# A fused cross-attention and maxout kernel: seven output pieces at the end, states-stationary scores, DMA-turned states and a new order

## Chip, cores and metric

The kernel runs on one core of one Trainium2 chip. The metric is the device time of one execution in microseconds (us). The engines are called as the profile calls them: PE (TensorE, matmuls; PEld its weight loads), DVE (VectorE), ACT (ScalarE), POOL (GpSimd) and SP (SyncE, which here only issues DMAs). Each engine works through its own queue of instructions in the order in which the program lists them, and waits on semaphores for what others produce.

## The reference

Two blocks run after each other. The first is a cross attention between tokens and a few states, with one softmax in each direction, and the second is a maxout feed-forward layer over the result.

```
B, H, S, Ns, D = 8, 8, 512, 32, 64
scores  = (x @ state^T) / sqrt(D);  a  = softmax(scores);   xread = a  @ state      # [B,H,512,64]
scores2 = (state @ x^T) / sqrt(D);  a2 = softmax(scores2);  sread = a2 @ x          # [B,H, 32,64]
y = concat([xread, sread], axis=2) -> rows of 8*64 = 512 features                   # 4352 rows
h = max(y @ w1, y @ w2, y @ w3)                                                     # 768 features
out = h @ w_out                                                                     # float32, 4352 x 512
```

Inputs and output are float32; the kernel computes in bf16 with float32 sums.

## The kernel before

**The work.** Eight batches of 512 token rows are computed one after the other, with the work of neighbouring batches interleaved, and at the end the 256 state rows of all batches together. The product of the attention with the states is folded into the weights: instead of `(a @ state) @ w` the kernel computes `G = state @ w` for each batch (three matrices of 768 columns for each of two halves of the heads, 4608 columns in all) and then `a @ G`. So each batch has these steps, and each step has a short name in the order table:

- `lx`, `lxg`, `lxu`: load x, all heads, half of them, or half without a cast; `lst`: load two batches' states; `lw`, `lwo`: load weights.
- `xt`/`xtc` or `xtd`: turn (transpose) x on PE with a copy out, or by DMA from SP. `stc`, `stt`, `stp`: cast two batches' states, turn them on PE, place the turned states into the block-diagonal tile `bd`. `std` is a DMA in place of `stt`, there in the code before but not in the order.
- `sc`, `ex`: the scores of tokens against states, 16 matmuls with x as the standing weights, and the exponential on ACT. `sq`, `eq`, `etd`: the same scores with the states as the standing weights (the result lies turned), their exponential, and a DMA that turns the exponentials into the layout of `e`. These three are also there in the code before but not in the order.
- `sum`, `wt`: row sums and reciprocal on DVE; the weights `a`, mostly on POOL. `at`/`atc` or `atd`: turn `a` on PE or by DMA.
- `pad`, `sr`, `srs`, `srt`, `ap`: the other softmax direction, that is a padded copy of x on POOL, 32 small matmuls, a scaling on DVE, a DMA turn from SP, and a placement into the tile that holds all batches' state rows.
- `g`/`gc`, `gr`/`gq`/`grc`: a slice or a run of columns of `G` on PE in 64x32 array tiles, and the copy out of PSUM. Letters at the end of a step name the engine or engines (`A` ACT, `D` DVE, `P` POOL, `S` SP).
- `l1`, `m0`, `ma`, `mb`: layer one, six matmuls into three PSUM banks for 128 of the 768 features; then a copy of the first bank on ACT and two maxima on DVE. `l1s` is the same for the state rows.
- `l2`, `l2c`, `so`: layer two, six matmuls into one bank for 128 rows, the copy out, the store. `l2p`, `l2pc`, `sop` do the same for a range of the 512 output columns; they are used at the end of the program.
- `busy`: one matmul on zeros, to keep PE running at the start. `look` and `flag`: at the end the kernel checks that all softmax sums were in range. `look` works on DVE; `flag` is a small matmul (L575), a reduction (L577) and a comparison (L578) on DVE. `vl` (L583) then loads the flag into a register of each engine, and a branch (L674) skips a slow repeat of everything. `hold` is one more matmul on zeros and a copy (L591, L593).

**What sets the order.** Nothing is scheduled by rules: the string `PLAN` lists all steps in one order, and each engine's queue is that order cut down to its own instructions. `BANKS` and `PAIRS` say which PSUM bank each request gets, and `PLACES` which of the two to four SBUF buffers a tile gets. A step waits for the last reader of its bank or buffer.

**PSUM.** Before, four banks are given out singly and four in two pairs; a pair takes the scores of a batch or two runs of `G`, and then one instruction copies 1024 columns out of it.

**DMA queues.** POOL issues the loads of x and of the weights and most stores; SP issues the turns and a few stores; ACT loads the states and issues a few late stores. A DMA is issued only when the engine's queue reaches it and what it waits for is there.

**The end.** The last batch's output is computed in 12 pieces of 128 or 256 columns and the first half of the state rows' output in two.

Of the kernel before, what the change touches and what calls it, by code (L numbers as in the profile page):

```python
# [9 lines left out]
F32 = mybir.dt.float32  # L10
# [8 lines left out]
    lst 0 A; lxu 0 0 S; zero; clr 0; clr 1; clr 2; clr 3; warm; lxg 0 1; busy 1; xones 1; ident; busy 1;  # L19
    lxg 1 0; busy 1; busy 1; stc 0 D; busy 1; busy 1; busy 1; busy 1; busy 1; lxg 1 1; stt 0; busy 1; busy 1;  # L20
    cxu 0 0 D; xt 0 0; stp 0 A; busy 1; xt 0 1; lw 0 2 1; lw 0 1 0; xtc 0 0 D; sc 0 0; xones 0; lw 0 2 2;
    xtc 0 1 D; busy 1; busy 1; sc 0 1; xt 1 0; ex 0 0; ex 0 1; lw 1 3 0; sum 0 0; sum 0 1; xtc 1 0 A; busy 1;
    busy 1; xt 1 1; sc 1 0; xtc 1 1 D; ex 1 0; busy 1; busy 1; sc 1 1; lw 2 3 2; wt 0 1 D; lw 2 3 1; lw 3 4 0;
    wt 0 0 P; lw 3 6 2; at 0 0; sr 0; ex 1 1; sr 1; g 0 0; sum 1 0; wt 1 0 P; g 1 0; atc 0 0 A; at 0 1; at 1 0;
    gc 0 0 A; atc 0 1 A; g 1 1; sum 1 1; gc 1 0 D; atc 1 0 A; srs 0; srs 1; g 0 1; wt 1 1 P; at 1 1; gc 0 1 A;
    l1 0 0; atc 1 1 D; lst 1 A; m0 0 0; lst 3 A; gc 1 1 A; ma 0 0; lw 3 6 1; lw 4 6 0; lxg 2 1; lxg 2 0; l1 0 1;
    m0 0 1; lwo; mb 0 0; g 0 2; g 1 2; ma 0 1; l1 1 0; lst 2 A; gc 0 2 A; mb 0 1; m0 1 0; ma 1 0; l1 0 2;
    mb 1 0; gc 1 2 A; m0 0 2; ma 0 2; l1 1 1; m0 1 1; g 1 3; stc 1 P; mb 0 2; ma 1 1; g 0 3; mb 1 1; stt 1;
    gc 1 3 A; l1 1 2; gc 0 3 A; m0 1 2; stp 1 DA; ma 1 2; g 0 4; g 0 5; l1 0 3; gc 0 5 D; g 1 4; mb 1 2;
    gc 0 4 A; m0 0 3; gc 1 4 A; ma 0 3; gr 2 1792 2304; mb 0 3; l1 1 3; m0 1 3; grc 2 1792 2304 A; xtd 2;  # L30
    ma 1 3; l1 0 5; stc 2 P; g 1 5; gr 2 0 512; mb 1 3; m0 0 5; ma 0 5; l1 1 4; gc 1 5 A; gr 2 1280 1792;
    m0 1 4; grc 2 0 512 D; mb 0 5; gr 2 512 1024; ma 1 4; grc 2 1280 1792 AD; l1 0 4; m0 0 4; ma 0 4; stt 2;
    mb 0 4; sc 2 -; ex 2 -; grc 2 512 1024 D; stp 2 AD; stc 3 D; mb 1 4; l2 0 3; l2 0 0; l2c 0 3 A; l2c 0 0 A;
    sum 2 -; l2 0 1; ones; pad 2; lxg 3 0; lxg 3 1; wt 2 - P; stt 3; xtd 3; l2c 0 1 A; l1 1 5; pad 3;
    so 0 0 2 P; lx 4; m0 1 5; l2 0 2; ma 1 5; mb 1 5; stp 3 A; l2c 0 2 A; l2 1 0; gq 2 1024 1280; gr 3 0 512;
    gr 3 1792 2304; l2c 1 0 D; grc 3 1792 2304 D; gqc 2 1024 1280 A; grc 3 0 512 A; atd 2; sr 2; l2 1 1; srs 2;
    sc 3 -; l1 2 0; m0 2 0; ex 3 -; l2c 1 1 D; l2 1 3; ma 2 0; gq 3 1024 1280; so 0 2 4 P; gqc 3 1024 1280 A;
    l2c 1 3 A; gr 3 512 1024; gr 3 1280 1792; mb 2 0; sum 3 -; wt 3 - P; atd 3; xtd 4; srt 0; sr 3; srs 3;
    l1 2 1; m0 2 1; ma 2 1; l1 2 2; m0 2 2; mb 2 1; ma 2 2; l1 2 3; m0 2 3; mb 2 2; ma 2 3; l1 2 5; m0 2 5;
    mb 2 3; l2 1 2; grc 3 1280 1792 A; grc 3 512 1024 A; ma 2 5; mb 2 5; l2c 1 2 D; l1 2 4; so 1 2 4 P; m0 2 4;  # L40
    ma 2 4; lx 5; mb 2 4; so 1 0 2 P; pad 4; gr 4 1792 2304; gr 4 0 512; grc 4 1792 2304 AD; l2 2 0; l2 2 1;
# [38 lines left out]
    1032103210 3213201321 0312013201 3201320120 3120132103 1203120312 0310321031 2013210321 0321032132 0132103120  # L80
    1320132103 2103120120 1201320123 0123120123 0213012013 0130123102 2
"""
PAIRS = """
    0101010101 1001010010 0110101010 1010101010 10
"""
PLACES = """
# [657 lines left out]
```

## Time and profile before

| what | before |
|---|---|
| time, median of 3 executions | 152.52 us (152.26 to 152.56) |
| profiled execution, from the first to the last instruction | 150.5 us |
| time of the runs beyond that span | 2.0 us |
| PE busy | 145.1 us (96%) |
| DVE busy | 118.0 us (78%) |
| ACT busy | 83.2 us (55%) |
| POOL busy | 56.1 us (37%) |
| granted TensorE clock | 1.000 |
| moved by DMA | 22.29 MB, mean 148 GB/s |

The span does not hold what lies around the program on the chip, so a time is read as span plus 2.0 us. "Busy" leaves out register, branch and semaphore instructions; these are seen only when a line of the program is asked for by itself. In rows of groups, the two numbers behind `|` are the busy time in us and the mean duration of one instruction in ns. In the chain of waits each row gives the start, the length and the work that the end of the program had to wait for, in us.

### The profile page before, as it was taken

Reading aid. Unit: us, or ns where it says so; the run is one execution under the profiler, and the core shown is the slowest. Engines: PE = TensorE matmul, PEld = TensorE weight load, DVE = VectorE, ACT = ScalarE, POOL = GpSimd, SP = SyncE. Lnnn points to the kernel's source line nnn. Section 1 sums busy time; section 2 is a strip of 40 time slices with the busy share of each in tenths; the row PEclk is TensorE's granted clock in tenths of the full one; section 3 lists DMA queues with packets and bytes.
Section 4 is the critical chain, followed back from the end, with each engine's and each line's share of the span. In section 5 each row is a group of like instructions: output and inputs, shape, how many; then the busy total and the mean of one; then the engine's idle time right before and its main releaser. Section 6 shows DMA issues by size and latency. Waiting matters only on the chain.

```text
span 150.5 us, 3618 instructions
## 1 busy us (share of the span) xinstructions
PE 145.1 (96%) x1422; PEld 72.8 (48%) x1422; DVE 118.0 (78%) x202; ACT 83.2 (55%) x144; POOL 56.1 (37%) x78
## 2 busy tenths in 40 slices
PE   6998999999999999999999999999999999999991
PEld 2556443335444443444344434443444446689770
DVE  6488788999967899789978997899789888674443
ACT  3366888965654574457546764676466653332220
POOL 6996911090392507350735064506250200001500
PEclk9999999999999999999999999999999999999999
DMA  4999999949647996998399839983303340300555
GB/s 121 195 188 189 206 230 198 196 97 139 124 97 171 235 182 189 108 209 178 145 102 216 183 139 90 231 183 131 157 4 78 121 175 7 139 0 17 190 199 167
DMA packets 39108, 22.29 MB, mean 148 GB/s; under 512 B 23072, under 2 KB 36896, under 8 KB 39088
## 3 DMA queue, kind: packets, MB, share of 16 engines
q0 software_dynamic: 15872, 13.96, 49.3%
q1 hardware_dynamic: 21632, 6.69, 22.8%
q10 hardware_dynamic: 1584, 1.38, 3.2%
q8 instruction: 12, 0.20, 0.6%
q14 instruction: 8, 0.07, 0.2%
HBM read 15.20 MB, written 8.91 MB: 160 GB/s over the span
## 4 chain that ended last, share of the span: by engine, by line
PE 88%; DMA 5%; POOL 3%; issue 1%; DVE 1%; ACT 1%; POOLq 0%
PE pw L477 47%; PE po L514 25%; PE pg L427 6%; DMA w<-in_moe_w_dram 5%; PE po L532 4%; PE ps L305 2%; PE psr L391 2%; POOL w L217 1%; POOL x L206 1%; PE pgh L427 1%; ACT G L444 1%; PE pt L261 1%; DVE held L593 0%; PE idle L591 0%; PE pat L358 0%
## 5 line engine op out<-in xcount | busy, mean ns | idle before, releaser
L477 PE MATMUL pw<-aT,G 128*128 128x512 bf16 x288 | 66.7, 379 | 0.0
L492 ACT CAST t<-pw 128x512 bf16<-128x512 f32 (+1 forms) x54 | 30.5, 564 | 27.3 <-PE pw L477 26.4
L497 DVE TENSOR_TENSOR t<-t,pw 128x512 bf16<-128x512 bf16 (+1 forms) x54 | 35.3, 654 | 11.1 <-ACT t L492 8.9
L477 PEld LDWEIGHTS <-G 128*128 128x128 bf16 x288 | 27.1, 98 | 32.8 <-issue 2.1
L514 PE MATMUL po<-wout,ht 128*128 128x512 bf16 x168 | 39.7, 379 | 0.0
L505 DVE TENSOR_TENSOR ht<-t,pw 128x512 bf16<-128x512 bf16 x48 | 32.9, 686 | 4.5
L349 POOL TENSOR_TENSOR a<-e,rden 128x1024 bf16<-128x1024 bf16 (+1 forms) x9 | 14.6, 1622 | 27.2 <-ACT osb L526 11.1
L514 PEld LDWEIGHTS <-ht 128*128 128x128 bf16 x168 | 15.4, 98 | 19.0 <-issue 1.7
L548 POOL DMA_DIRECT2D out_dram<-osb x13 | 7.4, 571 | 27.5 <-ACT t L492 27.5
L466 ACT CAST G<-pg 128x1024 bf16<-128x1024 f32 (+1 forms) x17 | 14.7, 895 | 2.1 <-PE pg L427 2.1
L526 ACT COPY osb<-po 128x512 f32<-128x512 f32 x15 | 8.9, 592 | 9.1 <-PE po L514 9.1
L526 DVE COPY osb<-po 128x512 f32<-128x512 f32 x14 | 9.6, 688 | 3.9 <-PE po L514 3.8
L375 POOL COPY xp<-x 128x1024 bf16<-128x1024 bf16 x12 | 12.3, 1059 | 0.0
L313 ACT ACTIVATE e<-ps 128x1024 bf16<-128x1024 f32 (+1 forms) x10 | 8.5, 854 | 6.7 <-PE ps L305 6.7
L466 DVE CAST G<-pg 128x1024 bf16<-128x1024 f32 (+1 forms) x12 | 11.6, 995 | 0.0
L342 DVE TENSOR_REDUCE seen<-e 128x32 f32<-128x1024 bf16 (+1 forms) x10 | 10.0, 997 | 1.7 <-ACT e L313 1.7
L427 PE MATMUL pg<-w,bd 64*32 64x512 bf16 (+1 forms) x288 | 10.7, 362 | 0.4 <-DMA w<-in_moe_w_dram 0.2
L444 ACT CAST G<-pg 128x768 bf16<-128x768 f32 x10 | 8.0, 810 | 2.7 <-PE pg L427 2.5
L543 POOL DMA_DIRECT2D out_dram<-osb x4 | 2.2, 544 | 19.4 <-ACT osb L537 19.4
L249 PE MATMUL idle<-zero 128*128 128x512 bf16 x18 | 7.4, 506 | 1.8 <-DVE zero L225 1.3
L477 PE MATMUL pw<-atp,w 128*128 128x256 bf16 x72 | 8.7, 272 | 0.0
L217 POOL DMA_DIRECT2D w<-in_moe_w_dram x10 | 7.7, 782 | 0.0
(70 smaller groups left out, 112.1 us busy)
## 6 DMA issues: line engine op xcount, KB each, us to landing
out_dram<-osb POOLq DMA_DIRECT2D x12, 512.0 KB, 3.7
x<-in_x_dram POOLq DMA_DIRECT2D x4, 512.0 KB, 7.2
x<-in_x_dram POOLq DMA_DIRECT2D x7, 256.0 KB, 5.8
w<-in_moe_w_dram POOLq DMA_DIRECT2D x4, 256.0 KB, 7.5
w<-in_moe_w_dram POOLq DMA_DIRECT2D x2, 384.0 KB, 7.5
wout<-in_moe_w_out_dram POOLq DMA_DIRECT2D x1, 768.0 KB, 12.0
out_dram<-osb SPq DMA_DIRECT2D x3, 256.0 KB, 2.4
stf<-in_state_dram ACTq DMA_DIRECT2D x4, 128.0 KB, 5.3
```

The lines of the kernel that those rows point to most:

```text
L342: nc.vector.reduce_sum(out=den, in_=parity(e[b], g), axis=AX.X)
L349: times[c](out=parity(a[b], g).rearrange("p j g s n -> p j (g s) n"), in0=parity(e[b], g).rearrange("p j g s n -> p j (g s) n"), in1=rdens ...
L375: nc.gpsimd.tensor_copy(out=xp[b][:, :, :, g * (D + 1):g * (D + 1) + D], in_=v[:, g])
L427: nc.tensor.matmul(p(s, g), bd(b, 2 * s + g)[64 * g:64 * g + 64, g, :], f(w_sb[64 * g:64 * g + 64, s]), start=True, stop=True, tile_positi ...
L444: copier[c[g]](out=G[b][:, g:h, :, m * 128:m * 128 + 128], in_=p[:, g:h, 0:384].rearrange("p g (i f) -> p g i f", i=3))
L466: copier[c[g]](out=v[:, g:h], in_=p[:, g:h, 0:c1 - c0])
L477: nc.tensor.matmul(pw[i][:, 0:n], lhs(i, k), rhs(k), start=(k == 0), stop=(k == nk - 1))
L492: nc.scalar.copy(out=t0s[b, m][:, 0:n], in_=open_ps["l", b, m][0][:, 0:n])
L497: nc.vector.tensor_max(t1s[b, m][:, 0:n], t0s.pop((b, m))[:, 0:n], open_ps["l", b, m][1][:, 0:n])
L505: nc.vector.tensor_max(ht[b][:, m, :], t1s.pop((b, m))[:, 0:n], open_ps.pop(("l", b, m))[2][:, 0:n])
L514: nc.tensor.matmul(p, ht[b][:, m, tokens(b, j)], wout_sb[:, m, :], start=(m == 0), stop=(m == NM - 1))
L526: copier[c[i]](out=o[:, j, i * w:i * w + w], in_=p[:, i * w:i * w + w])
```

## The change

Six things are changed at once:

1. **The end.** Batch 7's output is computed in 7 pieces of 128 to 512 columns, the first half of the state rows' output in one.
2. **Scores of batches 4 to 7** use `sq`, `eq`, `etd` in place of `sc`, `ex`.
3. **States 4 to 7** (the pairs 2 and 3) are turned by `std`, a DMA from SP, in place of `stt` on PE.
4. **PSUM**: all eight banks are given out singly. The scores and each pair of runs of `G` take two banks, and two instructions copy them out. `gq` is gone, since all `gr` now work like it.
5. **The padded copy of x** has its two halves 66 columns apart instead of 65, and its column of ones is two columns wide.
6. **All orders are new**: `PLAN`, `BANKS` and `PLACES`. Among other things there are 25 `busy` instead of 18, 14 of them ahead of the first turn of states instead of 9; `flag` is the fourth step from the end instead of the 44th; and the stores of whole rows are spread over POOL, SP and ACT, so that POOL issues 30 DMAs instead of 39.

```diff
 PLAN = """
-    lst 0 A; lxu 0 0 S; zero; clr 0; clr 1; clr 2; clr 3; warm; lxg 0 1; busy 1; xones 1; ident; busy 1;
+    zero; lxu 0 0 S; xones 1; busy 1; busy 1; lxg 0 1; busy 1; lst 0 A; busy 1; busy 1; ident; xones 0; busy 1;
...
-    sop 7 0 256 384 S; hold; vl;
+    flag; sop 7 1 0 384 S; hold; vl;
 """
...
-    homes = {n: iter("".join(t.split())) for n, t in (("b", BANKS), ("w", PAIRS))}
+    homes = [iter("".join(BANKS.split()))]
...
     def scores(b, g=None):
+        if g is None:
+            ps = [bank([128, 2, 2, HS, Ns], F32, "ps") for _ in range(2)]
...
     def exps(b, g=None):
...
+        if g is None:
+            for i in range(2):
+                nc.scalar.activation(
+                    out=out[:, i], in_=ps[i].rearrange("p c g s n -> p c (g s n)"), func=AF.Exp, scale=scale)
...
     def scores_turned(b):
-        p = open_ps["sq", b] = two_banks([128, 2, 2, 2, 128], F32, "pst")
+        ps = open_ps["sq", b] = [bank([128, 2, 2, 128], F32, "pst") for _ in range(2)]
...
     def exps_turned(b):
         new(eT, b, [128, 2 * J * 128], "eT")
-        nc.scalar.activation(
-            out=eT[b], in_=open_ps.pop(("sq", b)).rearrange("q c i g t -> q (c i g t)"), func=AF.Exp, scale=scale)
+        for c, p in enumerate(open_ps.pop(("sq", b))):
+            nc.scalar.activation(
+                out=eT[b][:, c * 512:c * 512 + 512], in_=p.rearrange("q i g t -> q (i g t)"), func=AF.Exp, scale=scale)
...
-    def g_run(b, c0, c1, apart=False):
...
+    def g_run(b, c0, c1):
+        ps = open_ps["g", b, c0] = [bank([128, 512], F32, "pg") for _ in range(2)]
...
     def g_ran(b, c0, c1, c):
         new_g(b)
...
+        v = G[b].rearrange("p g i f -> p g (i f)")
+        for g, p in enumerate(open_ps.pop(("g", b, c0))):
+            copier[c[g % len(c)]](out=v[:, g, c0:c1], in_=p[:, 0:c1 - c0])
```

Two functions that the new order calls are the same in both kernels:

```
    def states_turn_dma(k):
        p = open_ps["st", k] = buffer([128, 4, 128], BF16, "stT", k)
        nc.sync.dma_start_transpose(out=p, in_=st[k].rearrange("p t c d -> p (t c d)"))

    def e_turn_dma(b):
        new(e, b, [128, J, 2, HS, Ns], "e")
        nc.sync.dma_start_transpose(out=e[b].rearrange("p j g s n -> p (j g) (s n)"), in_=eT[b])
```

**The end of DVE's queue.** These are DVE's last rows ahead of the branch, first of the kernel before, then of the changed kernel. `osb` is the output tile and `po` its bank, `hts` the hidden layer of the state rows, `nok` and `flag` the two steps of the range check, `held` the copy of `hold`.

```order
L577 TENSOR_REDUCE nok<-pst 128x1
L578 TENSOR_SCALAR flag<-nok 128x1
L497 TENSOR_TENSOR t_2396<-t_2386,pw_2372 128x256
L505 TENSOR_TENSOR hts<-t_2396,pw_2373 128x256
L526 COPY osb<-po 128x512
L537 COPY osb<-po 128x256 x2
L526 COPY osb<-po 128x512
L537 COPY osb<-po 128x128 x3
L593 CAST held<-idle 128x512
L583 TENSOR_LOAD flag
L674 COMPARE_AND_BRANCH
```

In the changed kernel the same engine ends so:

```order
L487 TENSOR_TENSOR t_2456<-t_2451,pw_2425 128x256
L495 TENSOR_TENSOR hts<-t_2456,pw_2426 128x256
L495 TENSOR_TENSOR hts<-t_2393,pw_2353 128x256
L516 COPY osb<-po 128x512
L527 COPY osb<-po 128x128
L567 TENSOR_REDUCE nok<-pst 128x1
L568 TENSOR_SCALAR flag<-nok 128x1
L583 CAST held<-idle 128x512
L573 TENSOR_LOAD flag
L666 COMPARE_AND_BRANCH
```

The two rows that make the flag stood ahead of nine instructions of other work, and now stand behind the last output copy. The lines L573, L567 and L568 of the changed kernel are L583, L577 and L578 of the one before. In POOL's queue the flag's load comes behind its last store in both.

**The middle of SP's queue.** This is SP from the turn of batch 5's x to that of batch 7's, first before. `xT`, `aT` and `ats` are the turned x, weights and state reads.

```order
L291 DMA_TRANSPOSE xT<-x_87 128x16x128
L366 DMA_TRANSPOSE aT<-a 128x8x128
L410 DMA_TRANSPOSE ats<-sr 128x128
L291 DMA_TRANSPOSE xT<-x_88 128x16x128
L366 DMA_TRANSPOSE aT<-a 128x8x128
L410 DMA_TRANSPOSE ats<-sr 128x128
L291 DMA_TRANSPOSE xT<-x_89 128x16x128
```

In the changed kernel the same stretch reads:

```order
L284 DMA_TRANSPOSE xT<-x_87 128x16x128
L284 DMA_TRANSPOSE xT<-x_88 128x16x128
L538 DMA out_dram<-osb 128x1024
L370 DMA_TRANSPOSE aT<-a 128x8x128
L339 DMA_TRANSPOSE e<-eT 128x8x128
L538 DMA out_dram<-osb 128x512
L284 DMA_TRANSPOSE xT<-x_89 128x16x128
```

The turned exponentials (`e<-eT`) and stores of output rows have come in between the turns, and the state reads' turns have moved behind this stretch.

More of the change, by code (lines that the diff above doesn't have):

```diff
@@ L80 @@
[L80 to L84, printed above, removed]
[4 rows of a table added]
 """
 PLACES = """
+    osb x00:0 0:1 1:2 2:0 3:2 4:1 5:0 6:2 7:1 s:0;
+    st 0:0 1:1 2:0 3:1;
     xT 0:0 1:1 2:2 3:0 4:1 5:2 6:0 7:1;
@@ L299, in scores @@
     def scores(b, g=None):
+        if g is None:
+            ps = [bank([128, 2, 2, HS, Ns], F32, "ps") for _ in range(2)]
+        else:
+            p = bank([128, J, 1, HS, Ns], F32, "ps")
+            ps = [p[:, 2 * i:2 * i + 2] for i in range(2)]
+        open_ps["s", b, g] = ps if g is None else [p]
         gs = (0, 1) if g is None else (g,)
-        p = open_ps["s", b, g] = (two_banks if g is None else bank)([128, J, len(gs), HS, Ns], F32, "ps")
         for jj in range(2):
```

230 lines of the change are left out of this document (104 added, 126 removed), and 4 rows, old and new, of the table BANKS.

## Prediction

> **What bounds the kernel now.** I read the page's busy times first, then busy time by stretch, then the chain of waits, and last the end of the program line by line. The page gives the shares of the engines over the whole span.
>
> ```profile
> PE 145.1 (96%) x1422; PEld 72.8 (48%) x1422; DVE 118.0 (78%) x202; ACT 83.2 (55%) x144; POOL 56.1 (37%) x78
> ```
>
> Busy time by stretch, with start, end and length, then PE, PEld, DVE, ACT and POOL, the granted clock and the DMA share:
>
> ```profile
> 15.88:146.98 131.10, 131.06 (x1224) 65.07 (x1222) 105.92 (x178) 74.95 (x131) 42.97 (x55) 1.00 0.71 145
> 64.54:79.79 15.25, 15.25 (x150) 6.82 (x150) 12.89 (x21) 9.07 (x16) 6.03 (x7) 1.00 0.89 160
> ```
>
> From the first layer-one matmul at 15.88 to the last output matmul, PE never waits for anybody: 131.06 of 131.10 us, at full clock. DVE, the next engine, has 12.89 of 15.25 us per batch, so it has room. In this middle only two things change the time: how much PE work there is, and whether the new order opens a gap. Ahead of it lies a start of 15.9 us, behind it an end of 3.5 us (146.98 to 150.5), and these two are the other places to look.
>
> **PE's work in the middle.** These rows are from the chain of waits: one batch's period, a turn of states, a stretch of layer one.
>
> ```profile
> 38.64 0.22 PE pt L261 x4
> 57.19 0.56 PE pg L427 x16
> 57.75 2.69 PE po L514 x12
> 61.74 0.47 PE ps L305 x16
> 63.50 0.23 PE pgh L427 x8
> 63.73 0.43 PE pg L427 x16
> 64.16 0.38 PE psr L391 x31
> 64.54 5.30 PE pw L477 x24
> ```
>
> A batch's scores (L305) cost 0.47 us. With the states standing they become 16 matmuls of 256 columns in the 64x32 array tiles in which the runs of G already work. There, two runs of 512 columns that follow another tiled step take 0.43, so 0.215 for eight matmuls of 512 columns, which run side by side; 16 matmuls of 256 are two such rounds of half length, 0.21 us. That is the nearest row, and I take it: 4 x (0.47 - 0.21) = 1.04 us less. At worst the new form costs what the old one did, and the gain is nothing.
>
> Two turns of states leave PE for a DMA: 2 x 0.22 = 0.44 us less.
>
> A change between plain and tiled steps has a price too. Two runs alone take 0.56, two runs behind another tiled step 0.43: entering costs 0.13. The 12 matmuls behind a tiled step take 2.69 where 12 at 0.215 take 2.59, and 24 take 5.30 for 5.18: leaving costs 0.10 to 0.12. The order of before has 16 such groups behind the first layer one, the new one 17: 0.23 more. The output pieces add up to the same columns, whatever their number, and the extra zero matmuls all lie ahead of layer one. The sum is -1.04 - 0.44 + 0.23 = -1.25 us.
>
> **What could open a gap.** With single banks, a pair of runs that one ACT or DVE instruction copied now takes two; scores likewise.
>
> ```profile
> L466 ACT CAST G<-pg 128x1024 bf16<-128x1024 f32 x12 | 11.7, 1024 | 0.0
> L466 DVE CAST G<-pg 128x1024 bf16<-128x1024 f32 x7 | 8.5, 1217 | 0.0
> L466 ACT CAST G<-pg 128x512 bf16<-128x512 f32 x5 | 2.9, 586 | 2.1 <-PE pg L427 2.1
> ```
>
> That is 2 x 586 - 1024 = 148 ns more per pair on ACT, some 3 us over all 30 pairs and the scores, on an engine with 6 us to spare in each batch of 15.25. Copies move from DVE to ACT and back in the new order; summed by such rows over the middle, DVE's work comes out the same in both orders. In return a bank comes free one copy earlier. I cost this at nothing; the cover is DVE's 2.4 spare us per batch. The turned scores put a DMA turn of the exponentials between ACT and the sums; the nearest row, of the same size, is the turn of `a`:
>
> ```profile
> aT<-a SPq DMA_TRANSPOSE x6, 2.9
> xT<-x SPq DMA_TRANSPOSE x6, 5.3
> ```
>
> So a batch's scores must start 2.9 us earlier, and the new order has them start a batch or more ahead of its first layer one. The tightest turn is x of batch 2: in SP's queue it now stands behind the turn of states 2. That one waits for a cast on ACT, which the steps ahead of it there put at about 29.5 us, and holds the queue for about 1 us itself. Issued near 31.1 and with 5.3 us, the turn of x lands near 36.4, and PE's work ahead of the scores ends at about 37. I cost it at nothing, and at up to 0.5 us if both turns slow each other.
>
> **The start.** Timeline rows of PE, POOL and ACT, and a row of the chain:
>
> ```profile
> 1.28 4.02 PE L249 MATMUL idle<-zero 128*128 128x512 bf16 x9 [1.28 <-DVE zero L225]
> 5.09 0.61 PE L261 MATMUL pt<-ident,st 128*128 128x128 bf16 x4
> 13.06 2.05 POOL L349 TENSOR_TENSOR a<-e,rden 128x512 bf16<-128x512 bf16 x2 [1.47 <-DVE rden L344]
> 14.02 0.80 ACT L444 CAST G<-pg 128x768 bf16<-128x768 f32 x1 [0.83 <-PE pg L427]
> ```
> ```profile
> 6.06 7.41 DMA w<-in_moe_w_dram
> 15.88 2.59 PE pw L477 x12
> ```
>
> Nine zero matmuls hold PE from 1.28 to 5.09, 0.42 each. Five more, at 0.42 while the clock is cold and half of that after it, put the first turn of states at 6.4 instead of 5.09, and the scores and exponentials behind it some 0.9 us later. G waits for weights that land at 13.47 in any case (6.06 + 7.41), and the new order has the same bytes ahead of them. The turns of batch 1's `a` are moved behind the first layer one, so that one starts earlier, near 15.3: G's copies on ACT run from 14.0, two slices of 0.4, then a turn's copy of 0.6. It ends at 16.6, and then the two turns wait for POOL's weights, which follow the later exponentials: 2.05 us from about 15.0, so to 17.05. PE idles some 0.3 us there and starts the second layer one at 17.35, where before it was at 15.88 + 1.30 = 17.18. That is +0.2 us; with the weights' landing and the late exponentials either way, -0.6 to +1.0.
>
> So the last output matmul ends near 146.95 + 0.2 - 1.25 = 145.9, 1.05 us earlier.
>
> **The end.** Here is what each queue does after its last work; these instructions are not counted as busy and were asked for by line. First DVE's last copy form and the flag's comparison, then POOL's load of the flag, its branch, its tidying up behind the branch, and its last drain; then SP's drain, and POOL's first drain at the start of the program.
>
> ```profile
> L537 DVE COPY osb<-po 128x128 f32<-128x128 f32 x4 | 1.2, 289 | 1.4 <-PE po L532 1.3
> L578 DVE TENSOR_SCALAR flag<-nok x1: 154/154/154, 140.0 to 140.0; 128x1 int32<-128x1 f32 x1
> L583 POOLq TENSOR_LOAD <-flag x1: 795/795/795, 140.7 to 140.7; - x1
> L674 POOLq EVENT_SEMAPHORE  x5: 17/42/43, 142.1 to 145.3; - x5
> L674 POOLq INC_SWDGE_SEM  x1: 967/967/967, 145.4 to 145.4; - x1
> L739 POOLq DRAIN  x3: 46/109/3247, 146.4 to 150.2; - x3
> L739 POOLq EVENT_SEMAPHORE  x4: 17/17/17, 149.7 to 150.4; - x4
> L739 SPq DRAIN  x3: 7/7/13, 149.3 to 149.9; - x3
> L728 POOLq DRAIN  x1: 184/184/184, 0.3 to 0.3; - x1
> L728 POOLq INC_SWDGE_SEM  x1: 27/27/27, 0.1 to 0.1; - x1
> ```
>
> POOL had its flag at 140.1, long before the last matmul. It loaded it (0.8 us from 140.7), branched, waited until 145.3 for its stores, spent 0.97 us in the instruction at 145.4, and then 3.25 us in the drain that starts at 146.4. The engines meet at 149.7, and the program is over at 150.5. So POOL's tidying up of over 4 us lies beside PE's last work and ends 0.3 us behind SP's drain at 149.3; it just about sets the end already.
>
> The new order makes the flag last. DVE's copy of the last piece ends 0.3 us after the last matmul, the reduction and the comparison follow, taken at 0.15 us each by the comparison's row, so with the gaps between them the flag is there at +0.7. All of POOL's chain is behind it: load, branch and five passed semaphores, +1.9 (140.7 to 142.1 and five at some 0.1); 0.97; the drain; and 0.85 from the meeting to the end. POOL's stores have long landed, so nothing else is waited for. For the drain the trace has two rows: 0.18 us where POOL had issued no DMA, and 3.25 after 39. If the drain has a fixed length it is 3.25; if it grows with the DMAs issued, 30 make 0.18 + 3.07 x 30/39 = 2.54. The rows don't tell which, and I take the middle, 2.9. The sum is 0.7 + 0.1 + 1.9 + 1.0 + 2.9 + 0.85 = 7.4 us from the last matmul to the end, where before it was 3.5: +3.9, or from +3.5 to +4.2.
>
> Altogether -1.05 + 3.9 = +2.85: a span of 153.35 instead of 150.5, and with the 2.0 us around it, which the median of 152.52 shows, 155.4 us.
>
> **The rivals.**
>
> *The drain only covers a wait for the others.* It ends 0.3 us behind SP's drain, which is close for chance, and then a late flag finds it short. Against it: the row shows no semaphore on it, and the engines meet in the event behind it. The load and the 0.97 us stay: 0.7 + 0.1 + 1.9 + 1.0 + 0.1 + 0.85 = 4.65, +1.15 over before, and with -1.05 the time is 152.6, within what can be told from no change. The Trainium skill ("VectorE: DVE Perf Modes", section "The DRAIN you can't avoid") says that the drains which the runtime puts around a kernel take a constant 12 ns or so on all engines, which would make this rival's case. Here SP's drains of 7 to 13 ns agree, and POOL's of 3247 ns doesn't.
>
> *Both the drain and the instruction ahead of it are short when POOL's stores have long landed.* At the program's start they take 0.18 and 0.03. Then the last stores set the end, as before. One of 64 KB from ACT lands in 1.8 us; in the new tail ACT copies a piece and issues two stores behind the last matmuls, so the last is issued near +0.7 instead of +0.4 and the end is at +3.9 instead of +3.5.
>
> ```profile
> out_dram<-osb ACTq DMA_DIRECT2D x3, 64.0 KB, 1.8
> ```
>
> That is 152.52 - 1.05 + 0.35 = 151.8, faster. It decides if the two records together are under 1 us in the new profile.
>
> *The new order opens gaps on top of it.* If x of batch 2, or a bank, makes PE wait 1 to 2 us, the forecast becomes 156.4 to 157.4.
>
> **How the numbers follow.** A difference under 0.2% (0.3 us) can't be told from no change here. The flag's late chain with the long drain has a chance of 0.62, at 155.4 and in a range of its own from 154.3 to 156.4: the drain gives -0.35 to +0.35, the start -0.8 to +0.8. The short drain has 0.20 (152.6, give or take 0.6: one third each to faster, same and slower); the short tidying up 0.13 (151.8); gaps on top 0.05. Slower is 0.62 + 0.05 + 0.03 to 0.07, faster 0.13 + 0.07, and the rest the same. The range reaches from the short tidying up, 151.7, to the upper end of the likeliest case, 156.4.
>
> **What would show it.** Right: POOL's load of the flag starts behind the last output copy, about 0.8 us after the last output matmul; its drain of 2.5 us or more follows about 3 us later; the span ends over 7 us behind that matmul, and the matmul itself ends near 145.9. Four turned scores take about 0.2 us each on PE. Wrong: a drain under 0.3 us at that place, or PE's idle time in the middle over 1.5 us, or a last matmul after 147.5.

## The result and the profile after

The changed kernel took 155.06 us (median of 5 runs: three at 155.03 to 155.06, the other two at 157.76 and 158.39), the kernel before 152.34 beside it: a ratio of 1.0173, with a 95% interval from 1.0147 to 1.0198. So it is slower by 2.7 us, or 1.7%. Ratios here and below leave out runs that lie over 1.5% above the fastest of the same kernel, while medians and ranges take all of them.

The profiled execution of that comparison, the run at 157.76, had a longer span, 156.0 us, than the runs that gave the median, about 153.2. The longest of PE's waits in it is one that the second profile of the same kernel (run e0_again, span 153.8) does not have: 2.29 us at 72 us for a turn of weights by DMA (total, times and longest, in us).

```profile
PE pw L467 <- DMA aT<-a: 2.3, 1, 2.3
```

The lines below are from the second profile.

Page and stretch, to compare with 145.1 of 150.5 us and with 131.06 of 131.10. The second fence has start, end and length, then PE, PEld, DVE, ACT and POOL, the granted clock and the DMA share:

```profile
PE 145.1 (94%) x1385; PEld 70.0 (46%) x1385; DVE 111.2 (72%) x204; ACT 86.3 (56%) x168; POOL 53.4 (35%) x74
```
```profile
15.98:147.16 131.18, 130.60 (x1188) 62.01 (x1187) 102.34 (x183) 77.21 (x154) 41.35 (x52) 1.00 0.78 153
```

PE is still busy nearly throughout, but no longer to the last 0.04 us. The start, by the timeline of PE:

```profile
1.27 6.14 PE L242 MATMUL idle<-zero 128*128 128x512 bf16 x14 [1.27 <-DVE zero L218]
7.22 0.42 PE L254 MATMUL pt<-ident,st 128*128 128x128 bf16 x4
...
15.98 1.46 PE L467 MATMUL pw<-aT,G 128*128 128x512 bf16 x6
17.27 0.39 PE L362 MATMUL pat<-ident,a 128*128 128x128 bf16 x4
17.82 0.40 PE L362 MATMUL pat<-ident,a 128*128 128x128 bf16 x4 [0.17 <-POOL a L353]
18.06 0.59 PE L467 MATMUL pw<-aT,G 128*128 128x512 bf16 x2
```

The fourteen zero matmuls hold PE until the first turn of states at 7.22, and the second layer one starts at 18.06, against 17.02 in the trace of before (17.18 in the prediction, which took it from the chain's row). The end, by line: the flag's comparison, then POOL's load of it, its branch, the instruction ahead of the drain, and the drains.

```profile
L568 DVE TENSOR_SCALAR flag<-nok x1: 153/153/153, 147.6 to 147.6; 128x1 int32<-128x1 f32 x1
L573 POOLq TENSOR_LOAD <-flag x1: 840/840/840, 147.8 to 147.8; - x1
L666 POOLq COMPARE_BRANCH  x1: 70/70/70, 148.7 to 148.7; - x1
L666 POOLq INC_SWDGE_SEM  x1: 791/791/791, 149.6 to 149.6; - x1
L730 POOLq DRAIN  x3: 46/109/2512, 150.4 to 153.5; - x3
```

Here POOL's load stands 0.6 us behind the last output matmul (147.16), where before it stood 6 us ahead of it, and its long drain runs alone: the last store landed at 149.55, before the drain starts.

All profiles of this study in one table, in us, worked out from their traces. "Middle" goes from the start of the second layer one to the end of the last output matmul, "waits" is the time in it in which PE did nothing, "landing" is when the last store landed and "tail" when the program ended, both counted from that matmul. The runs from e1 on are the experiments below, in their order. In the profiles marked * the records of 12 layer-two matmuls are missing; each leaves a false gap of 0.05 us, and these 0.63 us are not counted as waits.

| run | second layer one | middle | waits | landing | tail | span |
|---|---|---|---|---|---|---|
| before | 17.02 | 129.92 | 0.00 | +2.20 | 3.52 | 150.5 |
| changed, first profile * | 17.68 | 131.65 | 2.81 | +2.57 | 6.63 | 156.0 |
| changed (e0_again) | 18.06 | 129.10 | 0.41 | +2.39 | 6.64 | 153.8 |
| e1_flag_early | 16.91 | 131.29 | 2.43 | +3.87 | 5.22 | 153.4 |
| e2_before_flag_late | 16.77 | 129.94 | 0.00 | +2.19 | 7.40 | 154.1 |
| e3_ten_more | 17.68 | 133.74 | 3.19 | +2.46 | 7.64 | 159.1 |
| f1_store_moved * | 17.36 | 129.56 | 0.68 | +4.22 | 5.58 | 152.5 |
| f2_nine_idle * | 16.72 | 131.24 | 2.18 | +4.11 | 5.46 | 153.4 |
| f3_tokens_out * | 17.93 | 129.77 | 0.30 | +3.60 | 4.71 | 152.4 |
| g1_hold_last * | 17.84 | 130.20 | 1.36 | +2.69 | 4.04 | 152.1 |
| g2_hold_nine_sum * | 16.74 | 129.34 | 0.66 | +2.78 | 4.13 | 150.2 |
| g3_hold_tokens * | 16.66 | 130.57 | 0.96 | +2.82 | 3.93 | 151.2 |
| h1_before_std | 16.96 | 131.49 | 1.66 | +2.16 | 3.57 | 152.0 |
| h2_before_std_sq | 16.47 | 154.30 | 17.25 | +2.17 | 3.59 | 174.4 |

From before to the second profile of the changed kernel that is +1.04 at the start, -0.82 in the middle and +3.12 at the end: +3.34. To the first profile it is +0.66, +1.73 and +3.11. So the end is the same in both, and what makes one execution of this kernel longer than the other lies in the middle.

### The profile page after: what moved, and what is told of

Same layout as the page of the kernel before. It is cut to its first block, busy times and chain, and to the rows that moved or that the text cites. A ratio compares the mean times of both kernels' runs of the same rounds, so it can differ in the third digit from the quotient of the medians.

```text
span 156.0 us, 3539 instructions
## 1 busy us (share of the span) xinstructions
PE 142.9 (92%) x1371; PEld 69.6 (45%) x1385; DVE 111.5 (72%) x204; ACT 86.4 (55%) x168; POOL 53.6 (34%) x74
## 4 chain that ended last, share of the span: by engine, by line
PE 67%; DMA 10%; DVE 7%; POOL 5%; ACT 4%; issue 3%; DVEq 0%; POOLq 0%
PE pw L467 37%; PE po L504 18%; DMA w<-in_moe_w_dram 6%; PE pg L431 5%; PE po L522 4%; DMA aT<-a 4%; DVE t L487 3%; DVE ht L495 2%; ACT bd L264 2%; ACT t L482 1%; POOL w L210 1%; PE psr L395 1%; POOL a L353 1%; POOL xp L379 1%; POOL x L199 1%
## 5 line engine op out<-in xcount | busy, mean ns | idle before, releaser
L504 PE MATMUL po<-wout,ht 128*128 128x512 bf16 x156 | 38.8, 379 | 0.6
L459 ACT CAST G<-pg 128x512 bf16<-128x512 f32 (+1 forms) x40 | 20.7, 569 | 7.6 <-PE pg L431 7.6
L516 ACT COPY osb<-po 128x512 f32<-128x512 f32 x18 | 10.4, 596 | 7.5 <-PE po L504 7.5
L459 DVE CAST G<-pg 128x512 bf16<-128x512 f32 (+1 forms) x20 | 11.3, 598 | 3.6 <-PE pg L431 3.6
L538 POOL DMA_DIRECT2D out_dram<-osb x7 | 4.0, 574 | 28.5 <-ACT osb L516 28.5
L431 PE MATMUL pg<-w,bd 64*32 64x512 bf16 (+2 forms) x336 | 11.6, 350 | 1.3 <-DMA w<-in_moe_w_dram 1.3
L516 DVE COPY osb<-po 128x512 f32<-128x512 f32 x11 | 7.5, 686 | 2.8 <-PE po L504 2.5
L447 ACT CAST G<-pg 128x384 bf16<-128x384 f32 x18 | 8.0, 494 | 2.3 <-PE pg L431 2.3
L467 PEld LDWEIGHTS <-w 128*128 128x128 bf16 x72 | 7.0, 98 | 1.6
L431 PEld LDWEIGHTS <-bd 64*32 64x32 bf16 x336 | 3.6, 90 | 7.9 <-issue 5.8
```

The lines of the kernel that those rows point to most:

```text
L431: nc.tensor.matmul(p(s, g), bd(b, 2 * s + g)[64 * g:64 * g + 64, g, :], f(w_sb[64 * g:64 * g + 64, s]), start=True, stop=True, tile_positi ...
L459: copier[c[g % len(c)]](out=v[:, g, c0:c1], in_=p[:, 0:c1 - c0])
L467: nc.tensor.matmul(pw[i][:, 0:n], lhs(i, k), rhs(k), start=(k == 0), stop=(k == nk - 1))
L504: nc.tensor.matmul(p, ht[b][:, m, tokens(b, j)], wout_sb[:, m, :], start=(m == 0), stop=(m == NM - 1))
L516: copier[c[i]](out=o[:, j, i * w:i * w + w], in_=p[:, i * w:i * w + w])
```

## The experiments

Each time below is a median beside the kernel before on the same chip (152.1 to 152.3 us). The changed order spreads far more than the one before, as the waits below explain in part, so the profiles' stretches carry the verdicts, and the medians support them.

### The changed kernel again, and the flag in both kernels

The changed kernel with no edit:

> The changed kernel once more, with nothing edited, beside the experiments below on the same chip: 155.0 us by its first runs, a tail from the last output matmul to the end of 6.6 us (149.33 to 155.9 in its first profile), and so a last matmul near 146.6 where the span is 153.2. If the new order holds PE up in the middle, as the first profile shows it around 68 us, the row of PE's busy time from the first layer one on stays more than 1 us below that stretch's length here too; if not, it is within 0.3 us of it, as before.

It took 156.50 us (155.46 to 157.36) beside 152.22, a ratio of 1.0294 [1.0241, 1.0347] on this chip, where 155.0 was expected. The tail is 6.64 as in the first profile; the waits in the middle are 0.41 us, in this execution of 155.71. PE's busy time from the first layer one on stays 0.58 below that stretch's length, which is neither of the two cases expected. The long wait of the first profile lies at 72 us, not at 68.

The flag early in the changed kernel (its PSUM bank moves with it in `BANKS`):

```diff
-    sop 7 3 0 512 A; sop 7 2 0 512 S;
+    sop 7 3 0 512 A; flag; sop 7 2 0 512 S;
...
-    sop 7 0 0 128 A; flag; sop 7 1 0 384 S; hold; vl;
+    sop 7 0 0 128 A; sop 7 1 0 384 S; hold; vl;
```

> The changed kernel with the flag's matmul, reduction and comparison moved from the fourth step from the end to the 31st, and nothing else. My theory, that POOL's load, branch, tidying up and drain behind a late flag are what the change lost: the tail goes from 6.6 us back to 3.5 as in the kernel before, so 155.05 - 3.1 = 151.95 us, faster than the kernel before by 0.4. First rival, POOL's drain begins only once the last stores have landed, whenever the flag is there: 154.5 or more. Second rival, what was lost lies in the middle or the start: 155.0, no change.

It took 155.46 us (153.68 to 157.23), a ratio of 1.0149 [1.0099, 1.0199]: better than the changed kernel by more than a per cent, but far from 151.95. Two things stood in the way. First, the list of PE's waits in this profile begins with the same turn of weights by DMA:

```profile
PE pw L467 <- DMA aT<-a: 1.9, 1, 1.9
```

Second, the tail became 5.2, not 3.5, although POOL's drain had ended 5 us ahead of the program's end (it runs from 145.9 to 148.5, and the last output matmul ends at 148.2). So the first rival falls: the drain did not wait for the last stores. Now the stores were late, landing 3.9 us behind that matmul. So my theory held for POOL's chain, and was wrong that nothing else stood behind it; the second rival is right in part, since 1.85 us lie in the middle. Both leads are followed below.

The flag late in the kernel before:

```diff
-    l2p 7 3 0 256; flag; l2pc 7 1 0 128 A;
+    l2p 7 3 0 256; l2pc 7 1 0 128 A;
...
-    sop s 0 0 256 S; sop 7 0 256 384 S; hold; vl;
+    sop s 0 0 256 S; flag; sop 7 0 256 384 S; hold; vl;
```

> The kernel before with its flag moved to the place that it has in the changed kernel, behind the last output copy, and nothing else. My theory: the tail grows from 3.5 us by what stands behind the flag; with this kernel's own rows for POOL (0.97 for the instruction ahead of the drain, 3.25 for the drain with 39 DMAs) it is 6.6 + (0.97 - 0.79) + (3.25 - 2.51) = 7.5 us, so 152.35 + 4.0 = 156.35 us, slower than the changed kernel by 1.3. If the drain has one length for any late flag, the 2.51 of the changed kernel's first profile: 155.4. If the drain of 3.25 only covered a wait for the others: 153.5.

It took 156.01 us (155.88 to 156.17), a ratio of 1.025 [1.022, 1.028]. The start and the middle are those of before, and the tail is 7.40 for 7.5 expected. Its rows for POOL:

```profile
L583 POOLq TENSOR_LOAD <-flag x1: 692/692/692, 147.3 to 147.3; - x1
L674 POOLq INC_SWDGE_SEM  x1: 967/967/967, 149.0 to 149.0; - x1
L739 POOLq DRAIN  x3: 46/109/3247, 150.0 to 153.8; - x3
```

The drain lasts 3247 ns whether its start is early (before) or late (here), to the nanosecond, so it doesn't cover a wait for anybody. This one move costs 3.8 us, where the whole change costs 2.7 in the first comparison and 4.3 beside these runs.

Ten more DMAs on POOL:

```diff
-    so 6 0 1 P; so 5 0 4 P; so 6 2 3 A;
+    so 6 0 1 P; so 5 0 4 P; spare 0; spare 1; spare 2; spare 3; spare 4; spare 5; spare 6; spare 7; spare 8; spare 9;
+    so 6 2 3 A;
...
+    def load_spare(k):
+        nc.gpsimd.dma_start(out=spare[k], in_=state[0, k % 8])
```

> The changed kernel with ten more DMAs on POOL, each a load of 32 rows of 256 bytes into a tile that nobody reads, issued where POOL has nothing to do, some 7 us ahead of its last store. Theory A, the last drain grows by each DMA that POOL has issued: before, 3.07 us over the 0.18 at the program's start for 39 DMAs, changed, 2.33 for 30, so 0.078 each; the drain becomes 0.18 + 40 x 0.078 = 3.3 us, the instruction ahead of it about 0.97, and the time 155.05 + 0.8 + 0.2 = 156.0. Theory B, it grows with bytes or rows that were moved: these DMAs have 32 rows of the usual 128, so a quarter of it, 155.3. Theory C, its length has another cause: 155.05 and a drain of 2.5.

```profile
L671 POOLq INC_SWDGE_SEM  x1: 987/987/987, 153.9 to 153.9; - x1
L735 POOLq DRAIN  x3: 46/109/3329, 154.9 to 158.8; - x3
```

The drain is theory A's 3.3, and the tail is 1.0 us longer (7.64 for 6.64). With 30, 39 and 40 DMAs it took 2.512, 3.247 and 3.329: 0.082 us for each, (3.247 - 2.512) / 9 as well as (3.329 - 2.512) / 10. Small loads count as much as large stores, so theory B falls, and C with it. The time missed its 156.0: it was 160.27 (158.43 to 160.84), with 3.2 us of waits in the middle, 2.42 of them for the turn of weights, and PE's work 1.9 us longer than in the changed kernel. The granted clock accounts for most of that: it was 0.50 from 74.8 to 78.2 us, from the end of that wait on, and the six layer-one matmuls there took 2.74 us instead of 1.47. Behind the 2.29 us wait of the changed kernel's first profile it stayed at 1.00. The extra DMAs were issued from 139 to 144 us, long after the wait, so they did not cause it; why the time was longer than the changed kernel's in all four runs stays open, and I use this run for its tail alone.

### The store beside the turn of weights

In the profile with the early flag, SP issued batch 4's turn of `a` at 67.04, and POOL a store of 512 KB (not 1 MB, as the expectation below has it) at 67.48. First SP's row and its landing, then POOL's timeline:

```profile
L370 SPq DMA_TRANSPOSE aT<-a x1: 1548/1548/1548, 67.0 to 67.0; - x1
...
DMA to landing us min/median/max: 6.1/6.1/6.1
```
```profile
67.48 0.61 POOL L538 DMA_DIRECT2D out_dram<-osb  x1
68.08 0.92 POOL L194 DMA_DIRECT2D x<-in_x_dram  x1
```

The store was moved ahead of the two padded copies:

```diff
-    so 1 0 1 P; xtd 5;
+    so 1 0 1 P; so 0 2 4 P; xtd 5;
...
-    grc 5 512 1024 AD; so 0 2 4 P; grc 5 1280 1792 AD;
+    grc 5 512 1024 AD; grc 5 1280 1792 AD;
```

> The kernel with the early flag, and one store of POOL (batch 0's rows 2 and 3, 1 MB) moved ahead of the two padded copies of x that it stood behind; nothing else. In the profile with the early flag this store was issued at 67.48, 0.44 us behind SP's turn of batch 4's weights at 67.04; both landed at 73.17, so the turn took 6.1 us, and PE waited 1.85 us for it. In the profile of the changed kernel without that wait the turn had a lead of 1.0 us and took 4.4. My theory, that the two share the DMA engines: the turn is back at 4 to 4.5 us, PE's wait at 71 us is under 0.3, and the time is 155.3 - 1.85 = 153.5 us, with less spread than the 153.7 to 157.2 with the early flag alone. Rival, the turn is slow for its own reasons or those of the x loads: the wait stays, 155.3.

```profile
L370 SPq DMA_TRANSPOSE aT<-a x1: 1791/1791/1791, 67.2 to 67.2; - x1
...
DMA to landing us min/median/max: 3.8/3.8/3.8
```

The turn took 3.8 us and PE no longer waits there, as the theory has it. One profile would be weak evidence, as the changed kernel's second profile has no such wait either, but all of them agree. Where the store stands 0.26 to 0.44 us behind the turn (the changed kernel's first profile, the early flag, ten more DMAs), the turn takes 6.1 to 6.5 us and PE waits 1.85 to 2.42. Where it stands 1.0 behind (the second profile), the turn takes 4.4, and in the six profiles with the store moved 3.4 to 4.6, without a wait of PE for it. The median is 154.88 (153.70 to 155.56), above the expected 153.5 but with half the spread of the early flag alone. The tail stayed long: 5.58.

### The start, and the new scores

```diff
-    warm; stc 0 A; busy 1; cxu 0 0 A; busy 1; busy 1; busy 1; busy 1; stt 0;
+    warm; stc 0 A; cxu 0 0 A; stt 0;
```

> The same kernel as the one with the store moved, and besides only 9 zero matmuls ahead of the first turn of states, as in the kernel before, in place of 14. The clock opened between 4.2 and 6.9 us in the profiles so far; until then a zero matmul takes 0.42, afterwards 0.21. Theory: the first turn of states is at 4.7 to 5.1 us instead of 5.7 to 7.2, and the second layer one near 16.9, where the landing of the weights holds it (16.9 with the clock open at 4.2), so 0.0 to 1.1 us less than with 14: about 152.9 us. Rival, the matmuls are needed to open the clock: the first layer one comes later, and the time is 153.5 or more.

```profile
1.28 3.69 PE L242 MATMUL idle<-zero 128*128 128x512 bf16 x9 [1.28 <-DVE zero L218]
4.81 0.39 PE L254 MATMUL pt<-ident,st 128*128 128x128 bf16 x4
...
16.72 1.46 PE L467 MATMUL pw<-aT,G 128*128 128x512 bf16 x6
```

The start came out as expected: the first turn at 4.81 and the second layer one at 16.72, 0.64 us earlier than with fourteen. The time did not: 154.47 (154.20 to 155.33) for 152.9, though not for the rival's reason, as the first layer one was earlier. PE, earlier by that much, then waited elsewhere, 1.20 us of it at 65 us: DVE stood at the sums of batch 4, behind the DMA turn of the exponentials, with two maxima of batch 3 queued behind it and layer two waiting for those.

```profile
64.16 1.22 DVE L346 TENSOR_REDUCE seen<-e 128x32 f32<-128x1024 bf16 x1 [1.80 <-DMA e<-eT]
65.42 0.35 DVE L348 RECIPROCAL rden<-seen 128x32 f32<-128x32 f32 x1
65.69 1.22 DVE L495 TENSOR_TENSOR ht<-t,pw 128x512 bf16<-128x512 bf16 x2
```

The old scores in the new order:

```diff
-    sq 4; eq 4; etd 4;
+    sc 4 -; ex 4 -;
```
and the same for batches 5 to 7.

> The same kernel as the one with the store moved, with the scores of batches 4 to 7 computed as before the change (x standing, no turn of the exponentials by DMA) at the same places and in the same banks. Theory: PE has 4 x (0.47 - 0.21) = 1.04 us more work in the middle, where it waits for nobody, so 1.0 us longer than that kernel, 154.5. Rival, the turns of the exponentials cost as much in SP's queue as the scores save, or the new scores take longer than 0.21: 153.5 or less.

It took 154.50 us, a ratio of 1.0143 [1.0119, 1.0167], for 154.88 and 1.0165 [1.0134, 1.0197] with the new scores: no difference that can be told, so the rival is nearer. (The 154.5 that the theory named is hit only because the run that it starts from was 1.4 us longer than expected.) PE's work did grow, from 128.88 to 129.47 (middle less waits), but the waits shrank from 0.68 to 0.30. In this pair the new scores save PE 0.6 us net of their entries and exits, not 1.04, and longer waits give most of that back; that their turns cause these waits is argued, not shown.

### The branch of PE and the last stores

With the flag early, the zero matmul ahead of the flag's loads (`hold`) waited for nothing, since its bank 4 had long been read. PE took its branch 1.35 us before its last output matmul had ended. PE's branch, and ACT's two last stores with their times to landing, in the run with the store moved:

```profile
L666 PEldq COMPARE_BRANCH  x1: 739/739/739, 145.6 to 145.6; - x1
```
```profile
L533 ACTq DMA_DIRECT2D out_dram<-osb x2: 339/374/408, 147.0 to 147.4; - x2
...
DMA to landing us min/median/max: 3.7/3.8/4.0
```

The kernel before gives `hold` the bank that the last output copy reads. So, at the end of `BANKS`:

```diff
-    2517625013 4503415061 5031425603 7103652712 0534
+    2517625013 4503415061 5031425603 7103652712 0533
```

> The kernel with the early flag and the moved store, with one PSUM bank changed: the zero matmul ahead of the flag's loads takes the bank that the last output copy reads, so that PE can't pass it before that copy has ended, as in the kernel before. With the bank that the changed kernel gives it, it waited for nothing once the flag was early: PE's branch stood at 145.56, 1.35 us ahead of its last output matmul, DMA packets of instructions of 8 and 16 KB followed at 143.3, 143.8, 147.8 and 148.8, and the last stores landed 4.2 us behind the last matmul instead of 2.2 to 2.4. My theory, that fetched instructions hold up the one DMA engine of 16 that carries them and each store with it: with PE's branch at over 1 us behind the last matmul the 16 KB packet comes behind the stores, the last store lands at +2.3 to +2.8, the tail goes from 5.6 to 3.6 to 4.1, and the time from 154.9 to 153.2 us. Rival, POOL's early drain beside the stores is what slows them: landing and tail stay, 154.9.

```profile
L666 PEldq COMPARE_BRANCH  x1: 483/483/483, 149.3 to 149.3; - x1
```
```profile
L533 ACTq DMA_DIRECT2D out_dram<-osb x2: 338/374/411, 148.1 to 148.6; - x2
...
DMA to landing us min/median/max: 2.2/2.3/2.4
```

The same two stores land in 2.3 us instead of 3.8, and the tail is 4.04 instead of 5.58. POOL's drain begins 2.3 us ahead of the last output matmul in both, so the rival falls. The same holds over all profiles of this order with the flag early: with PE's branch 1.35 us ahead of that end the last store lands 3.6 to 4.2 us behind it (four profiles), with the branch 1.25 us behind it 2.7 to 2.8 (three). That PE's early branch makes the stores late is shown, as far as one edit can (DVE's branch moves by 0.36 us with it); that fetched instructions on one DMA engine are the means is argued from the packets (one of 16 KB begins 3.4 us ahead of the last landing in the first run, at 147.8, and 0.2 ahead of it in the second, at 150.5), not shown by itself. The time was 154.1 us, a ratio of 1.010 [1.0065, 1.0136], for 153.2 expected: 0.8 us of a wait for DVE at 65.7 is in the profile, as in the run with nine zero matmuls.

Both start edits on top of it:

```diff
-    sum 4 -; mb 3 5; mb 3 0;
+    mb 3 5; mb 3 0; sum 4 -;
```
and nine zero matmuls.

> The kernel of the run ahead of it with two more edits: 9 zero matmuls ahead of the first turn of states instead of 14, and the row sums of batch 4 two steps later in the order, behind two maxima of batch 3 (in the profile with 9 zero matmuls DVE waited 1.80 us for the DMA turn of the exponentials ahead of these sums, with PE's maxima queued behind, and PE waited 1.20 us for them). Theory: second layer one at 16.7, the middle 129.2, the tail 3.6 to 4.1 us: a span of 149.8, 151.7 us, faster than the kernel before by 0.6. Rival, other waits for DMA turns take the place: 152.5 or more.

It took 152.76 us (12 runs, 152.01 the shortest), a ratio of 1.0043 [1.0023, 1.0064]. The profile, of the run at 152.01, has the expected start (16.74) and middle (129.34); its last output matmul ends at 146.08, 0.86 ahead of before, and its tail of 4.13 gives 0.61 of that back. That run is the shortest of the twelve, so its profile is a favourable one; the median missed the 151.7, and that waits like those above still come and go in the others is likely, but no profile shows it. It is the fastest of the changed orders here and still slower than the kernel before.

With the old scores instead:

> The kernel with the bank changed, 9 zero matmuls at the start, and the scores of batches 4 to 7 as before the change, so without the DMA turns of exponentials. The profile with these scores and without the other two edits had the second layer one at 17.93, 129.77 us of middle and 4.71 of tail. Theory: 16.8 + 129.8 + 3.7 = 150.3 us of span, 152.2 us, level with the kernel before; so PE's gain by the new scores is nearly used up by what their turns make it wait. Rival, the new scores are worth their 1.04 us of PE: 152.9.

It took 154.38 us (152.94 to 155.19). Neither theory hit it; the profile, with a span of 151.2, has 0.8 us more of middle than expected, with a wait of 0.56 us for x of batch 2 at 37 us, where the run with fourteen zero matmuls had 0.13. Why the median is longer still is open. Beside the run ahead of it, which has the new scores and batch 4's sums two steps later, it is 1.6 us longer, and the intervals are apart (1.0134 to 1.0204 against 1.0023 to 1.0064). So whether the new scores pay seems to depend on what stands around them: here they do, in the pair before they did not.

### Two pieces of the change in the kernel before

```diff
-    stt 2; mb 0 4;
+    mb 0 4; std 2;
...
-    stt 3; xtd 3;
+    xtd 3; std 3;
```

> The kernel before with one piece of the change alone: the states of batches 4 to 7 turned by DMA from SP in place of PE, their placements some 30 steps later in the order. Theory: PE has 2 x 0.22 = 0.44 us less in a middle in which it waits for nobody, and the two DMA turns (3.6 to 4.1 us in the profiles of the changed kernel) lie in a stretch where SP's queue has room: 152.2 - 0.44 = 151.75 us. Rival, the turn of batch 3's x, or the turn of its weights behind it, comes later and PE waits: 152.2 or more.

`stp 2` and `stp 3` follow behind `l2 1 0` and `l1 2 0`. It took 153.49 us (152.77 to 154.50), a ratio of 1.0084 [1.0055, 1.0113]: the rival. SP's timeline shows why; ahead is the kernel before, behind it this one.

```profile
37.99 1.91 SPq L291 DMA_TRANSPOSE xT<-x  x1
41.98 1.23 SPq L366 DMA_TRANSPOSE aT<-a  x1
```
```profile
38.58 1.78 SPq L291 DMA_TRANSPOSE xT<-x  x1
40.45 1.81 SPq L265 DMA_TRANSPOSE stT<-st  x1
42.36 1.26 SPq L366 DMA_TRANSPOSE aT<-a  x1
```

The turn of `a` is issued only 0.4 us later, but with the states' turn in flight it takes 4.6 us to land instead of 2.7, and PE waits 1.59 us for it. The four matmuls saved at each turn were 0.22 us.

The scores as well:

```diff
-    sc 4 -; ex 4 -;
+    sq 4; eq 4; etd 4;
...
-    sum 4 -; srs 4;
+    srs 4;
...
-    mb 3 1;
+    mb 3 1; sum 4 -;
```
and the same for batches 5 to 7.

> The same, and besides the scores of batches 4 to 7 with the states standing, their exponentials turned by DMA, and the sums of each of these batches some eight steps later so that DVE doesn't wait for that turn. In the profiles of the changed kernel a batch's 16 new score matmuls took 0.34 us with the entry into the tiled form, and before 0.47. Theory A, the whole price is 0.34: 4 x 0.13 = 0.5 us less than the kernel with the states alone, 151.25. Theory B, 0.21 as I forecast: 1.04 less, 150.7. Rival, the turns of exponentials make DVE or PE wait, as in the changed kernel's order: 151.75 or more.

It took 176.51 us, and that is my order's fault: the state reads' matmuls (`sr`) read the exponentials too, and I left them where they were.

```profile
61.07 0.41 PE L323 MATMUL pst<-xT,bd 64*32 64x256 bf16 x16
61.42 1.47 PE L514 MATMUL po<-wout,ht 128*128 128x512 bf16 x6
...
68.34 0.45 PE L391 MATMUL psr<-xp,e 128*32 128x65 bf16 x32 [4.78 <-DMA e<-eT]
```

PE stood at them four times, 14.9 us in all, and at the end of three of these waits the granted clock fell to 0.5 for 3.4 to 6.8 us. The run still shows what the turned scores ask of an order: from them to the first reader of the exponentials 7.3 us pass here (61.07 to 68.34). And the scores between plain steps take 0.35 us (61.07 to 61.42), theory A's price.

## Why the prediction came true, and where it was wrong

The forecast was 155.4 us, and the measured 155.06 lies 0.3 beside it. The mechanism was the right one, the flag's late chain with the long drain: moving the flag alone makes the tail 7.40 in the kernel before, and moving it back takes POOL's chain off the end. That the number is so close is in part luck. In the second profile the end is 0.78 us under its forecast, the start 0.84 over and the gaps 0.41 over, which leaves 0.5 us; and the second set of runs of the same kernel has a median of 156.50, just above the range. Of the signs named, the load of the flag, the drain and the tail come out in their order, with a tail of 6.64 for "over 7"; but the last output matmul ends at 147.16 instead of near 145.9, and in the first profile two signs of being wrong are there, 2.8 us of waits in the middle (over 1.5) and a last matmul at 149.33 (after 147.5).

**The end, +3.9 forecast, +3.12 measured.** The flag's load was at +0.6 (0.8 forecast), load to the end of the waits 1.84 (1.9), the instruction ahead of the drain 0.79 (1.0), the drain 2.51 (2.9), the rest 0.85 (0.85). The term that was mis-sized is the drain, where I took the middle of two readings. It grows with POOL's DMAs, and the formula for that reading gave 2.54. By the Trainium skill ("VectorE: DVE Perf Modes", section "The DRAIN you can't avoid") the runtime's drains are constant and about 12 ns on all engines; POOL's last drain here is 2512, 3247 or 3329 ns by the number of its DMAs, so the measurement decides against it, and with it falls the rival of the short drain. The rival with both short falls by the same rows: 0.79 and 2.51 are far over 1 us together.

**What I had not seen at the end** is that the flag alone doesn't undo the loss. I wrote that POOL's stores have long landed and that nothing else is waited for. With the flag early the tail is 4.7 to 5.6, because PE then passes its branch early; with that mended too it is 3.9 to 4.1. The rest to 3.5 goes with the last stores, two of 128 and 64 KB that land in 2.2 to 2.4 us, where before they were three of 64 KB at 1.8.

**The middle's work, -1.25 forecast, -1.23 measured** (129.10 less 0.41 of waits, for 129.92). That it agrees to 0.02 is luck again: in the profile with the early flag it is -1.06. Its terms were sound: a group of new scores takes 0.23 us between tiled steps (73.29 to 73.52) for 0.21 forecast, and 0.35 with a plain step behind it, with the exits that I had put in a term of their own.

```profile
73.29 0.41 PE L326 MATMUL pst<-xT,bd 64*32 64x256 bf16 x16
73.52 0.40 PE L431 MATMUL pg<-w,bd 64*32 64x512 bf16 x8
73.84 0.45 PE L395 MATMUL psr<-xp,e 128*32 128x65 bf16 x32
```

**The gaps, 0 forecast, 0.41 measured here, 2.81 in the first profile and 0.3 to 3.2 in the profiles of this order with small edits.** This is the step that failed: "I cost this at nothing", with x of batch 2 named as the tightest turn. That one did bite in six of the profiles with small edits, 0.13 to 0.58 us at 37 to 38 us, about as bounded. But the larger waits were two that I had not looked for: the turn of `a` of batch 4, slowed by a store in POOL's queue, and DVE's sums behind the turn of the exponentials. I had read SP's queue for order and DVE for its mean spare time. The first misses what other queues have in flight, the second that a spare 2.4 us doesn't help when the instruction at the head of the queue waits for a DMA. The rival of gaps on top, to which I gave 0.05, describes the changed kernel's own first profile: its run took 157.76 us, and the rival had 156.4 to 157.4. So 0.05 was too little: two of the first five runs and two of the next four took over 157.2 us.

**The start, +0.2 forecast, +1.04 measured**, or +0.88 from the 17.18 of the prediction, which is near the bound of +1.0 worked out for it. The weights landed when I said (13.44 us in this profile, 13.47 before; in other profiles from 12.95 to 14.15). What I mis-sized is the zero matmuls: I took the clock to be open for four of the last five of them. In this profile all fourteen ran at 0.42 us, and the first turn came at 7.2 instead of 6.4; in others it came as early as 5.7. So with fourteen of them the start lies between -0.1 and +1.04.

## What to carry to other kernels

Ask of each flag, check or register load at a program's end what stands behind it in every engine's queue: POOL's tidying up costs some 0.1 us for each DMA that it ever issued, hidden only while PE still works. A turn by DMA is cheap for the engine that it leaves, but its landing depends on what all queues have in flight, so order its first reader on every engine by the slowest landing seen, not by the median. And when two costs end at about the same time, removing one shows the other: measure the end of each before counting a gain.

## What the runs showed of the hardware

Between 30 and 40 DMAs, POOL's last drain takes 0.06 + 0.082 us for each DMA that POOL has issued (30: 2.512, 39: 3.247, 40: 3.329), for loads of 8 KB as for stores of 512, and the instruction ahead of it 0.20 + 0.02 for each (0.791, 0.967, 0.987). Neither depends on when it starts: with the flag early and late they are the same to the nanosecond, with 39 DMAs and with 30.

The granted TensorE clock went up to 1.0 between 3.9 us (h2_before_std_sq) and 7.3 us (second profile of the changed kernel) into the span, while PE's zero matmuls start at 1.28 in every profile and are 0.43 us apart before it and 0.22 after. The Trainium skill ("TensorE: Matmul & The Clock Gate", section "Part 1: The HAM clock gate (the "warmup" mystery)") puts the transition around 4 us into sustained matmul activity, give or take 0.5 from run to run. Here it was 2.6 to 6.0 us, so a count of zero matmuls that is right in one run is too many in the next. In the middle it fell back to 0.5, for 3.4 to 6.8 us, at four waits of PE of 2.42 to 4.78 us; at four of 1.59 to 2.29 it did not.

When PE takes its branch ahead of its last matmul's end, this can cost the last stores 1.5 us of their landing (3.8 us for 2.3), with no wait for an engine to show for it. A turn by DMA of 128 x 1024 weights took 2.7 us to land in the kernel before, 4.6 behind another turn just issued, and 6.1 to 6.5 with a store of 512 KB issued 0.26 to 0.44 us behind it.
